# Where a fused attention and MLP kernel forms z and kv: at a step of their own, or at the head of the runs of sketches and numerators

## The chip, the cores and the metric

The kernel runs on one core of a Trainium2 chip. Its time is the device time of one execution in microseconds; 260.84 us is the median of three runs of the kernel before (260.82 to 261.14). One execution was also profiled. Engines are named as in the profile: PE is TensorE (PEld its weight loads), DVE is VectorE, ACT is ScalarE, POOL is GpSimd, SP is SyncE, which issues the DMAs.

## The reference

A linear attention with sketched second-order features, followed by an MLP with an exact GELU. Batch 4, heads 4, sequence 1088, head size 32, sketch size 8, hidden size 2048:

```python
a = einsum('rd,bhsd->bhsr', S1, x); b = einsum('rd,bhsd->bhsr', S2, x)
phi(x) = a_i * b_j                        # 8 x 8 = 64 features a token
kv  = einsum('bhsf,bhsd->bhfd', phi(k), v)   # per batch and head: 64 x 32
z   = sum over s of phi(k)                   # per batch and head: 64
num = phi(q) @ kv ;  den = phi(q) @ z + 1e-6
x   = num / den, heads side by side          # 4352 tokens x 128
out = gelu(x @ w_in) @ w_out                 # 128 -> 2048 -> 128
```

## The kernel before

The queries are handled in chunks of 512 tokens: chunk n is half of the first 1024 tokens of batch n // 2, eight chunks in all, and a ninth chunk (n = 8) holds the 64 last tokens of all four batches. The MLP is a list of steps `(n, fi)`: step t makes 128 hidden channels of one chunk (`hidden`, L686 to L699: TensorE into one of two PSUM banks `h_ps`, then the GELU on ScalarE). From step 32 on, chunk n has the sixteen steps 16 n to 16 n + 15. Four hidden blocks in a row form a block, for which GpSimd makes sums (`token_sums`, L741 to L744), and one or more steps later TensorE multiplies blocks and sums by `w_out` (`two_products`, L776), seven products in place of eight. When a chunk's products are done, VectorE and ScalarE take them from PSUM (`drain`, L788 to L797), and VectorE combines and turns them for the store (`combine` and `store`, L810 to L838).

Attention work is written into slots between these steps: `at(t, f, ...)` puts f behind the hidden step of t and ahead of the products of t. Each engine runs its instructions in the order of this text, by manual dependences between neighbours; nothing is reordered by a scheduler. For batch b from 1 on and chunk n the work is:

- `key_turn_blocks`, `features_of_all`, `outer_of_all`, `add_tokens`: the features `k_p` of the batch's keys and, on VectorE, their sums over eight tokens a lane, `k_s` (L969 to L975).
- `kv_sum` (L431): 36 matmuls with 128 rows and 32 columns, kv of each head transposed, one head in each quarter of the array. `z_sum` (L440): four matmuls of the same shape, `ones` against `k_s`, which put z of each head on its 32 lanes.
- `take_kv` (ScalarE copy) and `turn_kv` (two matmuls at 128 rows x 64 columns against the identity, then a ScalarE copy into `kz[b]`), for the numerators.
- `fold_z` calls `sketch_of_z` (L480): three short VectorE instructions contract z with the second sketch matrix and write the result into `S_abc[b]`, the stationary matrix of the query sketches.
- `query_turn(n)`, `query_sketch(n)` (L557: eight matmuls with 64 rows and 32 columns, `S_abc[b]` against the turned queries), `query_outer(n)` (L574: on VectorE, a, b and the denominator give the features divided by the denominator).
- `attend(n)` (L605): eight matmuls at 64 rows x 32 columns, `kz[b]` against the features; ScalarE copies the result to `xT`, which the hidden steps of chunk n multiply.

Batch 0 has a way of its own before the steps begin; its z is only needed in the form of `S_abc[0]` for the ninth chunk. `repeat_first_z` (slot 40) lays it out as `z_cols` on GpSimd (L496), and `turn_first_kv` turns it on TensorE and folds it.

The loop over n from 3 on puts the work in relation to t = 16 (n - 1), the first step of chunk n - 1. Before the change, kv and z of batches 2 and 3 stand together (`finish_keys` at t + 13 for n = 3 and 5), with the first z's turn behind them for batch 2, and `turn_kv` and the fold one slot later; two slots after kv, at t + 15, come the numerators of the chunk whose steps begin next and the sketch of the chunk after it (chunks 3 and 4 for batch 2). For batch 1, kv stands at slot 21, its turn at 22, z and its fold at 23, and the sketch of chunk 2 at 24.

Each call of `work_banks` takes the next of two pairs of PSUM banks (`w_ps`), and waits until what used that pair two calls ago is done.

Of the kernel before, what the change touches and what calls it, by code (L numbers as in the profile page):

```python
# [16 lines left out]
def kernel(  # L17
# [18 lines left out]
    pe, dve, act, pool, sp = nc.tensor, nc.vector, nc.scalar, nc.gpsimd, nc.sync  # L36
    B, H, S, D = q.shape
    R = S1.shape[0]
    F = R * R
# [3 lines left out]
    NP = H // 2  # L43
# [4 lines left out]
    CW = JC * 128  # L48
    G = 128 // 32
    NCH = J // JC  # L50
# [16 lines left out]
    def work_banks():  # L67

        return wps.tile([128, 2, CW], FP, name="w_ps")

    def work_bank():
        return work_banks()[:, 0]
# [7 lines left out]
    def out_bank():  # L80
        return ops.tile([128, CW], FP, name="o_ps")
# [137 lines left out]
    ident = big.tile([128, 128], FP, name="ident")  # L219
# [12 lines left out]
    ones = big.tile([128, D], FP, name="ones")  # L232
# [173 lines left out]
    k_s = {}  # L406

    def flat(features):
        return features.rearrange("p i j -> p (i j)")
# [16 lines left out]
    def kv_product(ps, lhsT, features, h, part, start=False, stop=False):  # L426

        pe.matmul(ps[h * D:(h + 1) * D, part * F:(part + 1) * F], lhsT=lhsT, rhs=features, start=start, stop=stop,  # L428
                  skip_group_check=True)

    def kv_sum(b, ps):  # L431


        for i in range(J):
            for h in range(H):
                kv_product(ps, main["v", b][:, h, i, :], k_p[b][h // 2][:, i, h % 2], h, 0, start=i == 0)
        for h in range(H):
            kv_product(ps, v_rem_aug[b][:, h, :], flat(k_p_rem[b % 2][:, h]), h, 0, stop=True)

    def z_sum(b):  # L440

        ps = held["kv"][:, 0]
        for h in range(H):
            kv_product(ps, ones, k_s[b][:, h], h, 1, start=True, stop=True)

    def fold_z(b):
        sketch_of_z(b, held["kv"][:, 0], F)

    kv_T = {}

    def take_kv(b, ps):
        kv_T[b] = att.tile([128, F], FP, name="kv_T")
        act.copy(out=kv_T[b], in_=ps[:, :F])

    def turn_kv(b, banks):

        for rows in (slice(0, 64), slice(64, 128)):
            pe.matmul(banks[rows, 1, :128], lhsT=kv_T[b], rhs=ident, start=True, stop=True)
        act.copy(out=kz[b], in_=banks[:, 1, :128])
# [20 lines left out]
    def sketch_of_z(b, ps, at):  # L480

        zs = att.tile([128, R, R], FP, name="z_s")
        dve.tensor_mul(out=zs, in0=ps[:, at:at + F].rearrange("p (i j) -> p i j", i=R), in1=sT[:, None, R:].broadcast_to([128, R, R]))
        c = ps[:, 2 * F:2 * F + R]
        dve.tensor_reduce(out=c, in_=zs, axis=mybir.AxisListType.X, op=AX.add)
        dve.tensor_mul(out=S_abc[b][:, :, :, 4:8], in0=c.rearrange("p (i f) -> p i f", i=2)[:, :, None].broadcast_to([128, 2, 2, 4]),
                       in1=own_r[:, None, :, None].broadcast_to([128, 2, 2, 4]))
# [11 lines left out]
    def turn_first_kv():  # L499

        ps, zs = work_bank(), held["zs"]
        for h in range(H):
            c, r = h // 2, h % 2
            pe.matmul(ps[h * D:(h + 1) * D, :F], lhsT=zs[:, r], rhs=ident[:, c * F:(c + 1) * F], start=True, stop=True)
        sketch_of_z(0, ps, 0)


# [44 lines left out]
    def batch_of(n, s, i):  # L552
        return n // NCH if n < NMAIN else i * 2 + s
# [51 lines left out]
    def attend(n, banks=None):  # L605


        W = width[n]
        m = 1 if n < NMAIN else B // 2
        banks = work_banks() if banks is None else banks  # L610
        f = qp[n].rearrange("f r x -> f (r x)")[:, :2 * W].rearrange("f (c i n r t) -> f c i n r t", c=NP, i=m, r=2, t=32)
        N = W // 2 // m
        for i in range(m):
            for s in range(2):
                rows, b = slice(s * 64, (s + 1) * 64), batch_of(n, s, i)
                for h in range(H):
                    pe.matmul(banks[h * D:(h + 1) * D, s, i * N:(i + 1) * N],  # L617
                              lhsT=(kz[b] if b else kz_first)[rows, h * D:(h + 1) * D],
                              rhs=f[rows, h // 2, i, :, h % 2], start=True, stop=True)
        xT[n] = att.tile([128, CW], FP, name="xT", bufs=3)  # L620
        to = xT[n][:, :W]
        to = to.rearrange("p (s x) -> p s x", s=2) if m == 1 else to.rearrange("p (s t i) -> p s i t", s=2, i=m)
        act.copy(out=to, in_=banks[:, :, :W // 2] if m == 1 else banks[:, :, :W // 2].rearrange("p s (i t) -> p s i t", i=m))
# [238 lines left out]
    r = Rounding(SR)  # L862
# [12 lines left out]
    banks = [out_bank(), out_bank()]  # L875
# [59 lines left out]
    def at(t, f, *a):  # L935
        slots[t].append(lambda: f(*a))
# [40 lines left out]
    held = {}  # L977
# [11 lines left out]
    def features_rem(pair):  # L989
        key_features_rem(pair, held["rem"])  # L990

    def finish_keys(b, z=True):
        held["kv"] = work_banks()
        kv_sum(b, held["kv"][:, 0])
        if z:
            z_sum(b)
        take_kv(b, held["kv"][:, 0])

    def round_at(t, w, product_by=dve):
        r = []  # L1000
# [18 lines left out]
    at(17, add_tokens, 1)  # L1019
    at(18, channel_sums, 4)  # L1020

    at(21, finish_keys, 1, False)
    at(22, lambda: turn_kv(1, held["kv"]))
    at(23, z_sum, 1)
    at(23, fold_z, 1)
    at(23, query_turn, 3)
    at(24, query_sketch, 2)
    at(24, query_outer, 2)
    for i, t in enumerate((25, 26, 28)):
        at(t, channel_sums, i)  # L1030
# [2 lines left out]
    for n in range(3, NCHUNK):  # L1033

        t = (n - 1) * NF
        b = (n + 1) // 2
        keys = n % 2 and b < B
        if n > 3:
            at(t - 6, query_turn, n)
        if keys:  # L1040
            at(t - 1, sketch_and_attend, n)
            at(t - 1, features_of_all, b)
        else:
            at(t - 1, attend, n - 1)
            at(t - 1, query_sketch, n)
        at(t - 1, query_outer, n)
        if keys:
            for r in range(2):
                at(t - 3 if n > 3 else t - 4, key_turn_blocks, b, r)

        if n == NMAIN:
            at(t + 15, attend, n)
        if keys:
            at(t + 5 + (n == NCH + 1), outer_of_all, b)
            at(t + 5 + (n == NCH + 1), add_tokens, b)
            at(t + 8, widen_v_rem, b)
            at(t + 13, finish_keys, b)
            if b == 2:
                at(t + 13, turn_first_kv)
            at(t + 14, lambda b=b: turn_kv(b, held["kv"]))  # L1060
            at(t + 14, fold_z, b)


    products = {t: [] for t in range(len(steps) + LAG)}
# [2 lines left out]
    for t, (n, fi) in enumerate(steps):  # L1067
# [13 lines left out]
        elif fi % NB == NB - 1:  # L1081
            b = fi // NB
# [11 lines left out]
    for t in range(len(steps) + LAG):  # L1094
        if t < 4:
# [9 lines left out]
            if t == 3:  # L1105
                banks = work_banks()
# [23 lines left out]
        if t < len(steps):  # L1130
            n, fi = steps[t]
            hidden(n, fi, by_halves=t >= 18 and (n < NMAIN or fi < 5))
        if t < len(steps) and steps[t][0] < NMAIN and steps[t][1] % NB == NB - 1:
            n, b = steps[t][0], steps[t][1] // NB
# [50 lines left out]
```

## Time and profile before

| | |
|---|---|
| median of the runs | 260.84 us |
| profiled execution | 260.86 us |
| span of the profiled execution | 259.1 us |
| clock granted to TensorE | 0.999 |
| `kv_sum` and `z_sum` (L428), first and last start | 51.3 and 151.5 us |
| sketches (L568) of chunks 2 to 7, first and last start | 57.1 and 183.2 us |
| numerators (L617) of chunks 2 to 7, first start | 69.0 us |
| fold of z (L483, L485, L486), median of each instruction | 224, 228 and 174 ns |

The span runs from the first to the last instruction that the profiler saw; the time of an execution is some 1.8 us longer. A row of the timeline gives the start, the length, the engine and line, what is written from what, the tile of the array (rows*columns) and the shape, and the number of rows merged (each fp32 matmul shows as two passes). Neighbouring passes overlap, so the cost of a group is read from its start to the start of the next group, and not from its length. A bracket at the end gives idle time before it and what ended that time.

### The profile page before, as it was taken

The page shows a single profiled execution, that of the slowest core. Times are in us where ns is not written, and L with a number is a line of the kernel's source. Part 1 is how long each engine was busy: PE and PEld are TensorE (multiplying, and loading weights), DVE is VectorE, ACT ScalarE, POOL GpSimd, SP SyncE. Part 2 cuts the span into 40 slices and gives each one's busy share as a digit, 9 for nine tenths or more (in the row PEclk, how much of TensorE's full clock was granted, in tenths as well). Part 3 has the DMA queues.
Part 4 walks back from the last instruction along what each step waited for, and adds up shares of the span by engine and source line. Part 5 has one row for each costly group of instructions (what it writes and reads, how often), then busy time and mean ns, then how long its engine had stood idle before and what let it go on. Part 6 is the DMA issues. An engine that isn't in the chain of part 4 may idle for free.

```text
span 259.1 us, 5758 instructions
## 1 busy us (share of the span) xinstructions
PE 254.6 (98%) x2335; PEld 134.8 (52%) x2335; DVE 151.6 (59%) x313; ACT 114.9 (44%) x221; POOL 163.5 (63%) x173
## 2 busy tenths in 40 slices
PE   8999999999999999999999999999999999999994
PEld 7856444344444554444444454444445444445794
DVE  2886879969698997680178957630565043600330
ACT  4675767432625333533335334533353335334431
POOL 3404006799968776687758766867768776877200
PEclk9999999999999999999999999999999999999999
DMA  6469849820000101001000011020001100010020
GB/s 205 137 192 360 206 95 220 217 54 13 3 0 13 30 4 28 13 12 31 3 0 3 0 27 17 3 41 0 3 0 25 19 4 0 14 29 0 3 41 20
DMA packets 29530, 13.48 MB, mean 52 GB/s; under 512 B 21824, under 2 KB 27712, under 8 KB 29504
## 3 DMA queue, kind: packets, MB, share of 16 engines
q1 hardware_dynamic: 29472, 13.12, 20.8%
q8 instruction: 18, 0.29, 0.5%
q14 instruction: 8, 0.07, 0.1%
q10 hardware_dynamic: 32, 0.00, 0.0%
HBM read 10.88 MB, written 2.23 MB: 51 GB/s over the span
## 4 chain that ended last, share of the span: by engine, by line
PE 98%; ACT 0%; issue 0%; DVE 0%
PE h_ps L692 45%; PE o_ps L776 33%; PE o_ps L827 5%; PE w_ps L824 3%; PE w_ps L428 2%; PE w_ps L857 1%; PE w_ps L617 1%; PE w_ps L568 1%; PE o_ps L417 1%; PE w_ps L534 1%; PE h_ps L706 1%; PE h_ps L333 1%; PE w_ps L945 1%; PE w_ps L635 0%; PE w_ps L333 0%; PE h_ps L373 0%
## 5 line engine op out<-in xcount | busy, mean ns | idle before, releaser
L692 PE MATMUL h_ps<-xT,w_in 128*64 128x512 f32 (+3 forms) x514 | 137.1, 576 | 0.0
L699 ACT ACTIVATE block<-h_ps 128x512 f32<-128x512 f32 (+1 forms) x128 | 73.0, 571 | 120.2 <-PE h_ps L692 119.8
L776 PE MATMUL o_ps<-block,w_out 128*64 128x256 f32 x224 | 57.5, 379 | 0.0
L692 PEld LDWEIGHTS h_ps<-xT,w_in 128*64 128x64 f32 (+1 forms) x514 | 41.9, 142 | 29.2 <-issue 11.6
L741 POOL TENSOR_TENSOR bits_low<-block 128x512 f32<-128x512 f32 x28 | 35.6, 1273 | 27.6 <-ACT block L699 27.6
L776 PEld LDWEIGHTS o_ps<-block,w_out 128*64 128x64 f32 x224 | 30.5, 137 | 37.5 <-issue 26.7
L742 POOL TENSOR_TENSOR bits_a<-block 128x512 f32<-128x512 f32 x28 | 35.7, 1276 | 12.8 <-ACT block L699 12.8
L743 POOL TENSOR_TENSOR bits_e<-bits_a,block 128x512 f32<-128x512 f32 x28 | 36.1, 1290 | 2.2
L744 POOL TENSOR_TENSOR bits_m<-block,bits_e 128x512 f32<-128x512 f32 x28 | 35.8, 1280 | 2.2
L580 DVE STREAM_TRANSPOSE w_ps<-w_ps 128x512 f32<-128x512 f32 (+1 forms) x7 | 4.9, 693 | 42.8 <-PE w_ps L568 30.1
L776 PE MATMUL o_ps<-bits_low,small 128*64 128x256 f32 x112 | 29.0, 381 | 0.0
L776 PE MATMUL o_ps<-block,small 128*64 128x256 f32 x112 | 28.9, 381 | 0.0
L776 PE MATMUL o_ps<-bits_a,small 128*64 128x256 f32 x112 | 28.8, 379 | 0.0
L776 PE MATMUL o_ps<-bits_m,w_out 128*64 128x256 f32 x112 | 28.7, 379 | 0.0
L776 PEld LDWEIGHTS o_ps<-block,small 128*64 128x64 f32 x112 | 15.0, 137 | 17.6 <-issue 10.2
L791 DVE COPY sums<-o_ps 64x256 f32<-64x256 f32 x8 | 3.3, 416 | 34.4 <-PE o_ps L776 34.4
L776 PE MATMUL o_ps<-bits_e,small 128*64 128x256 f32 x112 | 17.1, 384 | 0.0
L827 PE MATMUL o_ps<-g,w_out 128*128 128x512 f32 (+1 forms) x34 | 16.5, 572 | 0.0
L776 PEld LDWEIGHTS o_ps<-bits_m,w_out 128*64 128x64 f32 x112 | 15.3, 137 | 0.0
L776 PEld LDWEIGHTS o_ps<-bits_a,small 128*64 128x64 f32 x112 | 15.2, 137 | 0.0
L776 PEld LDWEIGHTS o_ps<-bits_low,small 128*64 128x64 f32 x112 | 15.0, 137 | 0.0
L776 PEld LDWEIGHTS o_ps<-bits_e,small 128*64 128x64 f32 x112 | 7.5, 136 | 10.6 <-issue 9.1
(181 smaller groups left out, 303.2 us busy)
## 6 DMA issues: line engine op xcount, KB each, us to landing
out_dram<-oT SPq DMA_DIRECT2D x26, 64.0 KB, 2.2
block<-in_moe_w_in_dram SPq DMA_DIRECT2D x3, 512.0 KB, 7.2
block<-in_moe_w_out_dram SPq DMA_DIRECT2D x3, 512.0 KB, 11.6
k<-in_k_dram SPq DMA_DIRECT2D x12, 128.0 KB, 2.8
v<-in_v_dram SPq DMA_DIRECT2D x12, 128.0 KB, 3.4
q<-in_q_dram SPq DMA_DIRECT2D x24, 64.0 KB, 2.3
k<-in_k_dram SPq DMA_DIRECT2D x2, 256.0 KB, 2.8
q<-in_q_dram SPq DMA_DIRECT2D x2, 256.0 KB, 4.1
```

What stands on the lines that cost most here:

```text
L428: pe.matmul(ps[h * D:(h + 1) * D, part * F:(part + 1) * F], lhsT=lhsT, rhs=features, start=start, stop=stop, skip_group_check=True)
L580: dve.transpose(out=tok, in_=ps[:, :, :H2])
L692: pe.matmul(ps[rows, :W], lhsT=w[:, rows], rhs=xT[n][:, :W], start=True, stop=True)
L699: act.activation(out=g_of[n, fi][:, :W], in_=ps[:, :W], func=ACT.Gelu)
L741: pool.tensor_sub(out=s[3], in0=a11, in1=a21)
L742: pool.tensor_add(out=s[1], in0=a21, in1=a22)
L743: pool.tensor_sub(out=s[2], in0=s[1], in1=a11)
L744: pool.tensor_sub(out=s[4], in0=a12, in1=s[2])
L776: pe.matmul(acc[n][bank][half * 64:(half + 1) * 64, col:col + HW], lhsT=fixed, rhs=moving, start=opens and e == 0 and name in "4715", stop ...
L791: dve.tensor_copy(out=N[lo, 0, one], in_=a0[lo, one])
L824: pe.matmul(o_of[n][i][:, :128], lhsT=g[:, i * 128:(i + 1) * 128], rhs=w_tile(w_out_sb, fi), start=first, stop=final)
L827: pe.matmul(o_of[n][:, cols], lhsT=w_tile(w_out_sb, fi), rhs=g[:, cols], start=first, stop=final)
```

## The change

Three things are changed. z and kv of batches 1 to 3 move to the head of the run that holds the numerators and the sketch: z first, then its fold on VectorE, then kv, then (for batches 2 and 3) the numerators of the chunk before, then the sketch. z gets a pair of banks of its own, and kv and the numerators share one pair: kv lies in the second half of the second bank. `turn_kv` moves to two slots after kv. The first z's turn takes two matmuls with 64 columns in place of four with 32, and stands three slots earlier, alone. (In the changed file, L503 is the first z's turn.)

```diff
     def z_sum(b):
-        ps = held["kv"][:, 0]
+        held["z"] = work_bank()
         for h in range(H):
-            kv_product(ps, ones, k_s[b][:, h], h, 1, start=True, stop=True)
+            kv_product(held["z"], ones, k_s[b][:, h], h, 0, start=True, stop=True)
     def fold_z(b):
-        sketch_of_z(b, held["kv"][:, 0], F)
+        sketch_of_z(b, held["z"], 0)
...
     def turn_first_kv():
         ps, zs = work_bank(), held["zs"]
-        for h in range(H):
-            c, r = h // 2, h % 2
-            pe.matmul(ps[h * D:(h + 1) * D, :F], lhsT=zs[:, r], rhs=ident[:, c * F:(c + 1) * F], start=True, stop=True)
+        for c in range(NP):
+            pe.matmul(ps[c * F:(c + 1) * F, :F], lhsT=zs.rearrange("f r d -> f (r d)"), rhs=ident[:, c * F:(c + 1) * F],
+                      start=True, stop=True)
         sketch_of_z(0, ps, 0)
...
-    def finish_keys(b, z=True):
-        held["kv"] = work_banks()
-        kv_sum(b, held["kv"][:, 0])
-        if z:
-            z_sum(b)
-        take_kv(b, held["kv"][:, 0])
+    def kv_and_attend(b, n):
+        banks = held["kv"] = work_banks()
+        kv_sum(b, banks[:, 1, CW // 2:])
+        if n >= NCH:
+            attend(n, banks)
+        take_kv(b, banks[:, 1, CW // 2:])
...
-    at(21, finish_keys, 1, False)
-    at(22, lambda: turn_kv(1, held["kv"]))
-    at(23, z_sum, 1)
-    at(23, fold_z, 1)
+    at(24, z_sum, 1)
+    at(24, fold_z, 1)
     at(23, query_turn, 3)
+    at(24, kv_and_attend, 1, 1)
     at(24, query_sketch, 2)
+    at(26, lambda: turn_kv(1, held["kv"]))
     at(24, query_outer, 2)
...
     for n in range(3, NCHUNK):
         t = (n - 1) * NF
-        b = (n + 1) // 2
+        b = (n + 1) // 2 if n % 2 else n // 2
         keys = n % 2 and b < B
...
         else:
-            at(t - 1, attend, n - 1)
+            if n % 2 == 0 and b < B:
+                at(t - 1, z_sum, b)
+                at(t - 1, fold_z, b)
+                at(t - 1, kv_and_attend, b, n - 1)
+                at(t + 1, lambda b=b: turn_kv(b, held["kv"]))
+            else:
+                at(t - 1, attend, n - 1)
             at(t - 1, query_sketch, n)
...
             at(t + 8, widen_v_rem, b)
-            at(t + 13, finish_keys, b)
             if b == 2:
-                at(t + 13, turn_first_kv)
-            at(t + 14, lambda b=b: turn_kv(b, held["kv"]))
-            at(t + 14, fold_z, b)
+                at(t + 10, turn_first_kv)
```

## The prediction

> **What bounds the kernel now.** I read the page first: shares by engine, then the chain of waits.
>
> ```profile
> PE 254.6 (98%) x2335; PEld 134.8 (52%) x2335; DVE 151.6 (59%) x313; ACT 114.9 (44%) x221; POOL 163.5 (63%) x173
> PE 98%; ACT 0%; issue 0%; DVE 0%
> ```
>
> TensorE is busy for 98% of the span and is 98% of the chain; no other engine has a share. So only what makes TensorE's stream of matmuls shorter, or puts a hole into it, counts. The profiled execution took 260.86 us, its span 259.1; the median of the runs shown is 260.84, so sums made against the profile carry over as they are.
>
> Busy is not streaming, so next I read TensorE's timeline around batch 2's kv, by start times: the distance from one start to the next is what a group costs.
>
> ```profile
> 93.31 1.03 PE L692 MATMUL h_ps<-xT,w_in 128*64 128x512 f32 x4
> 94.26 1.10 PE L428 MATMUL w_ps<-k_p,v 128*32 128x64 f32 x64
> 95.18 0.29 PE L428 MATMUL w_ps<-k_p_rem,v_rem_aug 128*32 128x64 f32 x8
> 95.29 0.29 PE L428 MATMUL w_ps<-k_s,ones 128*32 128x64 f32 x8
> 95.40 0.29 PE L504 MATMUL w_ps<-ident,z_cols 128*32 128x64 f32 x8
> 95.63 0.43 PE L776 MATMUL o_ps<-block,small 128*64 128x256 f32 x1
> ...
> 95.89 0.38 PE L776 MATMUL o_ps<-block,small 128*64 128x256 f32 x1
> ...
> 97.40 0.39 PE L458 MATMUL w_ps<-ident,kv_T 128*64 128x128 f32 x4
> 97.62 0.38 PE L776 MATMUL o_ps<-block,w_out 128*64 128x256 f32 x1
> ...
> 98.48 1.03 PE L692 MATMUL h_ps<-xT,w_in 128*64 128x512 f32 x4
> 99.44 0.66 PE L617 MATMUL w_ps<-q_pT,kz 64*32 64x256 f32 x16
> 99.90 0.64 PE L568 MATMUL w_ps<-qT,S_abc 64*32 64x256 f32 x16
> 100.47 0.65 PE L776 MATMUL o_ps<-bits_e,small 128*64 128x256 f32 x4
> 100.95 1.03 PE L692 MATMUL h_ps<-xT,w_in 128*64 128x512 f32 x4
> ```
>
> Undisturbed, a hidden step (L692 x4) takes 0.86 us, a pair of products 0.215 and eight passes at 128x32 0.11. The rest is paid at each change of tile shape. For kv: 0.10 before it (94.26 - 93.31 - 0.86, rounded up), 0.04 in its first group (0.92 for 64 passes that would need 0.88), 0.11 after its last (95.63 - 95.40 - 0.11), 0.045 in the next product: 0.295. For the 64x32 run: 0.10 before, 0.03 in the first group (0.46 against 0.43), 0.135 after (0.57 against 0.43), 0.045 in the next product: 0.31.
>
> **What the Trainium skill says.** "TensorEngine Tiling (Array Packing)", section Tiling Modes, says that a change of the tiling mode, unlike a change of tile, drains TensorE. The trace agrees: attend and sketch use eight tiles of one shape with nothing lost between them, and each change of shape costs the above. "SBUF — State Buffer", section Who interferes with whom, says that a VectorE instruction with two SBUF inputs and a GpSimd instruction that reads SBUF lock each other out for a whole instruction. The trace agrees: L811 takes 1.41 us beside L744, and 0.42 as its median.
>
> **The change part by part.** Call a stay in another shape an excursion.
>
> *Batch 1.* Before: kv (128x32), z (128x32) and the sketch (64x32) are three excursions at 51.2, 54.4 and 57.0: 0.295 + 0.285 (0.10 + 0.14 + 0.045 around z) + 0.31 = 0.89. After: one run 128x64 to 128x32 to 64x32 to 128x64. Entry 0.10 + 0.04, exit 0.135 + 0.045, and in the middle a change from 128x32 to 64x32 that no row of before shows. Bounds: nothing if tiles that only split their rows needn't drain; 0.20 if it is a little dearer than any seen. The nearest row changes the rows alone, from 64x64 to 32x64: L635's first 32 passes take 0.49 us (start 12.11 to 12.60), the second 32 take 0.57 before L534 at 13.17, with the drain. At 0.014 each that is 0.12 of drain. I take 0.12 + 0.03 of slow first passes = 0.15. The run then costs 0.47, saved 0.42.
>
> *Batches 2 and 3.* Two excursions each, 0.605, become one of 0.47: 0.135 each. Saved in all 0.42 + 0.27 = 0.69. The passes of z and kv, the numerators, the sketches and turn_kv (0.22, 97.40 to 97.62) are the same in number; turn_kv stays at 128x64 between a hidden step and products.
>
> *The first z's turn.* Its eight passes cost 0.11 inside kv's run. Now four at 128x64 stand alone between a hidden step and products, in the shape of their neighbours. Bounds: 0.11, as in kv's run, and 0.22, as L458's four passes of twice the columns. L399's four 64-column passes at 128x64 took 0.16 (10.00 to 10.16); I take that: 0.05 dearer. It reads z_cols, which GpSimd finishes at 88.42; the turn comes after the hidden step that starts at 88.57, at 89.43: covered by 1.0 us.
>
> *Hidden steps without cover.* In batch 1, before, kv stands between the fourth and fifth of six hidden steps that have no products between them, and gives ScalarE time. After, all six run back to back. ScalarE is behind there:
>
> ```profile
> 50.52 0.60 ACT L699 ACTIVATE block<-h_ps 128x512 f32<-128x512 f32 x1 [0.40 <-PE h_ps L692]
> 51.01 0.58 ACT L804 COPY g<-o_ps 128x512 f32<-128x512 f32 x1
> 51.48 0.62 ACT L699 ACTIVATE block<-h_ps 128x512 f32<-128x512 f32 x1
> ```
>
> There are two hidden banks. The fifth step would start at 51.17 and waits for the activation that ends at 51.12, the sixth at about 52.13 for that which ends at 52.10. From such an end to the next matmul took 0.15 (49.26 to 49.41). So 0.10 + 0.14 = 0.24 lost, between 0.1 and 0.4. GpSimd's sums are in time even so: bits_e, needed about 1.7 us earlier than the 55.66 of before, is done at 53.21.
>
> *The fold.* Before, VectorE's three instructions that make S_abc from z lie far ahead of the sketch. Now the sketch waits for them with only kv (and attend) between.
>
> ```profile
> 54.96 0.22 DVE L483 TENSOR_TENSOR z_s<-w_ps,sT 128x64 f32<-128x64 f32 x1 [0.92 <-PE w_ps L428]
> 55.21 0.23 DVE L485 TENSOR_REDUCE w_ps<-z_s 128x8 f32<-128x64 f32 x1
> 55.55 0.17 DVE L486 TENSOR_TENSOR S_abc<-w_ps,own_r 128x16 f32<-128x16 f32 x1
> ```
>
> z's first matmul was at 54.50, so with R as the run's start the fold begins at R + 0.46 and ends at R + 1.22. In batch 1 TensorE reaches the sketch at R + 0.04 + 0.11 + 0.99 (72 passes of kv) + 0.12 = R + 1.26; with 0.11 from an end to a weight load (49.26 to 49.37) the sketch can start at R + 1.33. Lost 0.08; bounds 0 and 0.3. Queued behind the waiting sketch are all later products and hidden steps. The turn of chunk 3's queries, now ahead of the fold on VectorE, runs from 54.04 to 54.75, before z's end. In batch 3 VectorE is idle from 151.9 and attend adds 0.46: no wait. In batch 2 VectorE has a backlog: k_s ends at 93.05, then the first z's fold (now 0.70 earlier in the queue), the query turn, L810, L811, L813 and the output turn, which ended at 97.84. Moved by at most 0.70 it ends at 98.54. The run starts at about 98.48 - 1.505 (kv's stay) - 0.22 (turn_kv) + 0.16 + 0.96 = 97.9, z is ready for the fold at 98.4, the fold ends near 99.25, the sketch is due at 99.6. No wait, with 0.3 to spare.
>
> *Other queues.* SP and GpSimd issue the same in the same order. ScalarE copies xT before kv_T, so the next hidden step waits as before: xT ended at 100.79, its weight load came at 100.85.
>
> **Sum.** 0.69 saved - 0.05 - 0.24 - 0.08 = 0.32 us. 260.86 - 0.32 = 260.54; I say 260.5, 0.1% faster.
>
> **Rivals.**
> 1. *Shape changes are cheaper than I price them, or the stalls don't come.* With the middle change free 0.45 more is saved; with half the two stalls 0.16. 260.86 - 0.32 - 0.45 to - 0.61: 259.9 to 260.1. For it: nothing measures this change. Against: the rows-only change drained too.
> 2. *The holes eat it all.* If the hidden steps lose 0.4 and the sketch 0.25, the gain is 0.69 - 0.05 - 0.65, nothing: 260.9. For it: ScalarE's queue is full just there.
> 3. *Slower, by the fold of batch 2.* If VectorE comes to L813 (two SBUF inputs) after GpSimd has begun the next L741, about 97.0 in the new order, it is locked out for 1.27 us, the output turn ends at about 99.6, the fold at 100.3, and the sketch due at 99.6 stands for 0.8 us: 260.54 + 0.8 = 261.3, and 261.6 if batch 1's fold is late by 0.3 too. It decides as soon as L813 starts 0.6 us later than before (96.41). For it: a 0.70 us fold is put ahead in this very queue, and L810 and L811 are already slowed. Against: L810 waits for GpSimd anyway until 94.67, which swallows the move.
>
> That the change doesn't do what it says is excluded: the new program has z, kv, numerators and sketch next to one another.
>
> **How the numbers follow.** Forecast (260.2 to 260.8) 0.48, rival 1 0.25, rival 2 0.13, rival 3 and other waits 0.14. Predicted 260.5. The range leaves out a tenth on each side: 259.9 to 261.2. No change means within 0.2%, 0.52 us, about what can be told here: 260.32 to 261.36. Faster: rival 1 and the lower edge of the forecast, 0.29. Slower: the upper part of rival 3, 0.11. Within: 0.60.
>
> **What will show it.** Right: from the first kv matmul's last group to attend's first start some 0.12 us more than the passes need; batch 1's sketch start less than 0.1 us behind the drain; VectorE's fold of batch 2 ended before attend has been issued. Wrong: attend right behind kv without a gap, or a weight load of the sketch that waits for VectorE for more than 0.3 us, or a hole in the hidden steps of batch 1 of over 0.4.

## The result and the profile after

The changed kernel takes 260.4 us in the median (259.74 to 260.87), the kernel before, measured together with it, 260.81; the ratio is 0.9983, with a 95% interval of 0.9976 to 0.9991. That is 0.43 us less, 0.17%. Measured once more, in a later set of runs, it gave 0.9982 (0.9974 to 0.9990).

The page's shares by engine, and its chain of waits:

```profile
PE 254.2 (98%) x2331; PEld 135.0 (52%) x2331; DVE 150.8 (58%) x313; ACT 114.8 (44%) x221; POOL 163.6 (63%) x173
PE 98%; ACT 0%; issue 0%; DVE 0%
```

TensorE has four passes fewer and is as full as before; nothing else has come into the chain. The span fell from 259.1 to 258.6 us. The start-up takes a little different time in every execution: the first hidden step at 128x64 begins at 47.53 us in the profile before and at 47.62 in the one after. So I measure from that step to the start of the last projection (L824, x16). That stage took 206.16 us before and 205.63 after: 0.53 us less. In a second profile of the changed kernel it took 205.63 again; the kernel before was profiled once.

TensorE's timeline around batch 1 (start, length, engine and line, tile, shape, rows merged):

```profile
47.62 5.69 PE L692 MATMUL h_ps<-xT,w_in 128*64 128x512 f32 x24
53.14 0.38 PE L776 MATMUL o_ps<-block,small 128*64 128x256 f32 x1
...
54.44 1.03 PE L692 MATMUL h_ps<-xT,w_in 128*64 128x512 f32 x4
55.39 0.32 PE L428 MATMUL w_ps<-k_s,ones 128*32 128x64 f32 x8
55.53 1.08 PE L428 MATMUL w_ps<-k_p,v 128*32 128x64 f32 x64
56.42 0.29 PE L428 MATMUL w_ps<-k_p_rem,v_rem_aug 128*32 128x64 f32 x8
56.69 0.67 PE L568 MATMUL w_ps<-qT,S_abc 64*32 64x256 f32 x16
57.29 0.43 PE L776 MATMUL o_ps<-block,w_out 128*64 128x256 f32 x1
```

and around batch 2:

```profile
88.43 1.03 PE L692 MATMUL h_ps<-xT,w_in 128*64 128x512 f32 x4
89.29 0.28 PE L503 MATMUL w_ps<-ident,z_cols 128*64 128x64 f32 x4
89.41 0.38 PE L776 MATMUL o_ps<-block,w_out 128*64 128x256 f32 x1
...
96.73 1.03 PE L692 MATMUL h_ps<-xT,w_in 128*64 128x512 f32 x4
97.68 0.32 PE L428 MATMUL w_ps<-k_s,ones 128*32 128x64 f32 x8
97.82 1.08 PE L428 MATMUL w_ps<-k_p,v 128*32 128x64 f32 x64
98.71 0.29 PE L428 MATMUL w_ps<-k_p_rem,v_rem_aug 128*32 128x64 f32 x8
98.94 0.66 PE L617 MATMUL w_ps<-q_pT,kz 64*32 64x256 f32 x16
99.39 0.64 PE L568 MATMUL w_ps<-qT,S_abc 64*32 64x256 f32 x16
99.96 0.65 PE L776 MATMUL o_ps<-bits_e,small 128*64 128x256 f32 x4
100.44 1.03 PE L692 MATMUL h_ps<-xT,w_in 128*64 128x512 f32 x4
```

The new change of shape is the step from kv's last group to the numerators. Eight passes need 0.11 us, and the next group starts 0.23 after (98.71 to 98.94): 0.12 of drain, the time in which TensorE starts nothing because the shape changes, and 0.02 more in the numerators' first passes. In batch 1 the step is 0.27 (56.42 to 56.69): the same drain and some 0.045 of waiting for the fold. The fold's last instruction and the sketch's weight loads, 0.12 after its end at 56.54:

```profile
56.37 0.17 DVE L486 TENSOR_TENSOR S_abc<-w_ps,own_r 128x16 f32<-128x16 f32 x1
56.66 0.21 PEld L568 LDWEIGHTS w_ps<-qT,S_abc 64*32 64x32 f32 x16
```

What lies around the matmuls of a run is then, for batch 1, 57.29 + 0.045 - 55.30 - 1.53 = 0.505 (the hidden step ends at 54.44 + 0.86 = 55.30, and 1.53 is what z, kv and the sketch need), against 0.89 in three excursions. For batch 2 it is 0.45, against 0.605; batch 3, read in the same way (153.48 to 156.34), has 0.46.

The first z's turn takes 0.12 us (89.29 to 89.41). The six hidden steps of batch 1 take 5.52 (47.62 to 53.14). Before, the first four took 3.64 (47.53 to 51.17), and two more would be 1.72: 0.16 is lost.

The gain adds up: 0.385 + 0.155 + 0.145 saved, less 0.01 for the turn and 0.16 for the hidden steps, is 0.515 of the 0.53.

### The profile page after: what moved, and what is told of

The parts are those of the page before. It is cut to its first block, busy times and chain, and to the rows that moved or that the text cites. A ratio compares the mean times of both kernels' runs of the same rounds, so it can differ in the third digit from the quotient of the medians.

```text
span 258.6 us, 5749 instructions
## 1 busy us (share of the span) xinstructions
PE 254.2 (98%) x2331; PEld 135.0 (52%) x2331; DVE 150.8 (58%) x313; ACT 114.8 (44%) x221; POOL 163.6 (63%) x173
## 3 DMA queue, kind: packets, MB, share of 16 engines
HBM read 10.88 MB, written 2.23 MB: 51 GB/s over the span
## 4 chain that ended last, share of the span: by engine, by line
PE 98%; ACT 0%; issue 0%; DVE 0%
PE h_ps L692 45%; PE o_ps L776 33%; PE o_ps L827 5%; PE w_ps L824 3%; PE w_ps L428 1%; PE w_ps L857 1%; PE w_ps L617 1%; PE w_ps L568 1%; PE o_ps L417 1%; PE w_ps L534 1%; PE h_ps L706 1%; PE h_ps L333 1%; PE w_ps L945 1%; PE w_ps L635 0%; PE w_ps L333 0%; PE h_ps L373 0%
## 5 line engine op out<-in xcount | busy, mean ns | idle before, releaser
L741 POOL TENSOR_TENSOR bits_low<-block 128x512 f32<-128x512 f32 x28 | 35.8, 1279 | 27.7 <-ACT block L699 27.7
L743 POOL TENSOR_TENSOR bits_e<-bits_a,block 128x512 f32<-128x512 f32 x28 | 36.1, 1291 | 2.2
```

Of the source, the lines that this page charges most:

```text
L741: pool.tensor_sub(out=s[3], in0=a11, in1=a21)
L743: pool.tensor_sub(out=s[2], in0=s[1], in1=a11)
```

## Experiments

A ratio stands against the kernel before, measured in the same set of runs; the bracket behind it is its 95% interval. The stage is that of the last section, read from each kernel's profile.

### Batch 1 alone, and all but batch 1

The first kernel puts batch 1's work back:

```diff
-    at(24, z_sum, 1)
-    at(24, fold_z, 1)
...
+    at(21, first_keys)
+    at(22, lambda: turn_kv(1, held["kv"]))
+    at(23, first_z)
+    at(23, lambda: sketch_of_z(1, held["kv"][:, 0], F))
     at(23, query_turn, 3)
-    at(24, kv_and_attend, 1, 1)
     at(24, query_sketch, 2)
-    at(26, lambda: turn_kv(1, held["kv"]))
```

`first_keys` (kv and its copy) and `first_z` write to one bank, as before the change.

> Batch 1 as before the change, the rest changed. Theory (each run of 128x32 and 64x32 work that is joined to another saves the changes of shape, about 0.15 us in batches 2 and 3, and about 0.38 in batch 1 less 0.16 lost between its hidden steps): gain over the kernel before 0.29 us of the 0.52 seen between the two profiles, so a profiled span of about 258.8 and no hole between the fourth and sixth hidden step near 51. Rival (batch 1's gain is eaten by the hidden steps, all of the gain is in batches 2 and 3): the same time as the changed kernel. Rival (the gain lies in z's own banks or in the earlier first turn, not in the shapes): also the same as the changed kernel.

Measured: 260.62 us in the median, 0.9990 (0.9982 to 0.9998). The stage took 205.86, 0.30 less than before. kv follows the fourth hidden step at 51.16, as it did.

The second kernel is the one before with the opposite edit: batch 1's z, fold, kv and turn at slots 24 and 26, z in its own banks, kv in the second half of a bank, and nothing else.

> Only batch 1 changed, all else as before, the first z's turn too. Theory: gain 0.22 us over the kernel before, all of it between 47 and 61 us. Rival (batch 1's gain is eaten by the hidden steps): no gain.

Measured: 260.31, 0.9986 (0.9979 to 0.9994). The stage took 205.93, 0.23 less. The two parts make 0.53, which is the whole. So batch 1's gain isn't eaten, and it doesn't come from the early turn of the first z, which this kernel lacks. It does have z in banks of its own, and so have batches 2 and 3 of the first kernel: no run separates this rival. But the profile before leaves it nothing to save: in batch 2 z follows kv's last group after 0.11, its bare passes (95.18 to 95.29), and in batch 1 it follows the hidden step after 0.10 (54.40 to 54.50), the price of the shape. The sum over changes of shape leaves nothing for it either. In the medians the two parts stand the other way round, 0.18 below the kernel before for the first kernel and 0.49 for the second. The two intervals overlap and hold the stages' 0.30 and 0.23, so the split rests on the stages, of which there is one profile for each kernel.

### The price of a change of shape

The first z's turn at its new place, with 32 columns:

```diff
-        for c in range(NP):
-            pe.matmul(ps[c * F:(c + 1) * F, :F], lhsT=zs.rearrange("f r d -> f (r d)"), rhs=ident[:, c * F:(c + 1) * F],
-                      start=True, stop=True)
+        for h in range(H):
+            c, r = h // 2, h % 2
+            pe.matmul(ps[h * D:(h + 1) * D, :F], lhsT=zs[:, r], rhs=ident[:, c * F:(c + 1) * F], start=True, stop=True)
```

> As changed, with the first z's turn in four matmuls with 32 columns at its new place, where its neighbours have 64. Theory: a stay of its own in another shape: 0.10 + 0.03 + 0.11 + 0.11 + 0.045, about 0.40 us from the hidden step's end to the products against 0.12: 0.28 us more. Rival (so short a stay hides behind the weight loads of its neighbours): 0.12 as with 64 columns.

TensorE's timeline of it:

```profile
88.45 1.03 PE L692 MATMUL h_ps<-xT,w_in 128*64 128x512 f32 x4
89.41 0.32 PE L504 MATMUL w_ps<-ident,z_cols 128*32 128x64 f32 x8
89.66 0.43 PE L776 MATMUL o_ps<-block,w_out 128*64 128x256 f32 x1
...
89.92 0.38 PE L776 MATMUL o_ps<-block,w_out 128*64 128x256 f32 x1
```

From the hidden step's end (89.31) it takes 0.35 to the products, and the first product 0.26 in place of 0.215: 0.395 against 0.12. The stage took 205.91, 0.28 more than the changed kernel; the median was 260.57, 0.9990 (0.9982 to 0.9998). The same passes, whose share inside a run of their own shape was 0.11, cost 0.28 us more where they stand alone. This is what the 64 columns of the changed kernel avoid.

The next run was to double the change between 128x32 and 64x32, by putting kv between the numerators and the sketch:

```diff
-        kv_sum(b, banks[:, 1, CW // 2:])
         if n >= NCH:
             attend(n, banks)
+        kv_sum(b, banks[:, 1, CW // 2:])
```

> As changed, but in batches 2 and 3 the numerators stand between z and kv: two more changes between 128x32 and 64x32 in each run, the same matmuls. Theory: each change costs 0.14 us, 0.28 a batch, 0.56 us in all over the changed kernel: about 261.0, no gain left. In the timeline 0.11 to 0.12 between the last passes of one shape and the first of the next. Rival (such a change is nearly free, since only the rows are split): less than 0.1 us.

Measured: 262.41, 1.0065 (1.0050 to 1.0081), the stage 2.23 longer than in the changed kernel. Neither theory had this:

```profile
97.29 0.32 PE L428 MATMUL w_ps<-k_s,ones 128*32 128x64 f32 x8
97.54 0.66 PE L617 MATMUL w_ps<-q_pT,kz 64*32 64x256 f32 x16
98.95 1.10 PE L428 MATMUL w_ps<-k_p,v 128*32 128x64 f32 x64 [0.74 <-ACT xT L623]
99.87 0.29 PE L428 MATMUL w_ps<-k_p_rem,v_rem_aug 128*32 128x64 f32 x8
100.09 0.66 PE L568 MATMUL w_ps<-qT,S_abc 64*32 64x256 f32 x16
```

kv now waits until ScalarE has copied the numerators, whose second bank it shares (in another half of its columns, but this program orders the two by bank): it starts at 98.95, and by its passes and drain it would have started at about 98.11 (97.54 + 0.46 + 0.11). That is 0.84 of the 1.12 us by which each of the two runs is longer; the rest is the two changes. Two of them can still be read: z to numerators, 0.25 for eight passes that need 0.11 and whose first group costs 0.03 more, so 0.11; kv to sketch, 0.22 for eight passes, so 0.11. It also shows why kv stands ahead of the numerators in the shared banks.

So the doubling was tried again without that wait: z a second time, into an idle bank of its own pair, between the numerators and the sketch of batches 2 and 3:

```diff
+    def z_again(b):
+        for h in range(H):
+            kv_product(held["z2"][:, 1], ones, k_s[b][:, h], h, 0, start=True, stop=True)
...
                 at(t - 1, kv_and_attend, b, n - 1)
+                at(t - 1, z_again, b)
```

> As changed, with z of batches 2 and 3 made a second time, into an idle bank, between the numerators and the sketch: eight passes at 128x32 and two more changes of shape (64x32 to 128x32 and back) in each run, and no new wait for another engine. The earlier run that was to double these changes was confounded by a wait for ScalarE. Theory: 0.11 for the passes and 0.14 for each change, 0.39 a batch, 0.78 in all over the changed kernel: about 261.2. Rival (a change that only splits the rows is nearly free): the passes alone, 0.22 in all, about 260.6.

Measured: 261.49, 1.0026 (1.0019 to 1.0033), the stage 1.15 longer than in the changed kernel, 0.57 in each run:

```profile
98.58 0.66 PE L618 MATMUL w_ps<-q_pT,kz 64*32 64x256 f32 x16
99.17 0.32 PE L428 MATMUL w_ps<-k_s,ones 128*32 128x64 f32 x8
99.58 0.67 PE L569 MATMUL w_ps<-qT,S_abc 64*32 64x256 f32 x16
```

and its weight loads:

```profile
98.58 0.18 PEld L618 LDWEIGHTS w_ps<-q_pT,kz 64*32 64x32 f32 x16
99.17 0.16 PEld L428 LDWEIGHTS w_ps<-k_s,ones 128*32 128x32 f32 x8 [0.41 <-issue]
99.58 0.18 PEld L569 LDWEIGHTS w_ps<-qT,S_abc 64*32 64x32 f32 x16 [0.25 <-PE w_ps L428]
```

From the numerators to z there is 0.59 for what needs 0.46: 0.13 of drain. From z to the sketch there is 0.41; 0.11 are the passes and 0.14 what such a change and the slow first passes cost elsewhere, and the bracket names a further wait: the sketch's pair of banks is the one that z has just written, and TensorE waits there for its own matmuls to end. That is the 0.16 to 0.18 a run beyond the 0.39 expected; it is what is left over, and no run measures it alone. The free change is refuted; the total isn't a clean measure of its price, but the step from the numerators to z is.

### How much the fold may be late

> As changed, with the fold of z done twice in a row in batches 1 to 3, the result being the same: 0.68 us more on VectorE ahead of the sketch. Theory: in batch 1 nothing covers it, the sketch comes about 0.65 later; in batches 2 and 3 the fold was done 0.42 us ahead of the sketch's weight loads, so about 0.35 each is exposed (0.68 less 0.42, and 0.1 for the wait). In all about 1.3 us, 261.7. Rival (VectorE has more to spare than that, since TensorE's own matmuls hold the sketch): no change in batches 2 and 3, 0.65 in all.

```diff
     def fold_z(b):
         sketch_of_z(b, held["z"], 0)
+        sketch_of_z(b, held["z"], 0)
```

Measured: 261.2, 1.0017 (1.0008 to 1.0025), the stage 0.90 longer than in the changed kernel: 0.60 in batch 1, 0.15 to 0.16 each in batches 2 and 3. Batch 1 is nearly as expected, the others show less than half. The fold of batch 2 on VectorE, its second time, in this kernel (the edit moves line numbers behind it by one), and then TensorE's weight loads:

```profile
98.77 0.21 DVE L484 TENSOR_TENSOR z_s<-w_ps,sT 128x64 f32<-128x64 f32 x1
99.01 0.23 DVE L486 TENSOR_REDUCE w_ps<-z_s 128x8 f32<-128x64 f32 x1
99.28 0.17 DVE L487 TENSOR_TENSOR S_abc<-w_ps,own_r 128x16 f32<-128x16 f32 x1
```

```profile
99.02 0.18 PEld L618 LDWEIGHTS w_ps<-q_pT,kz 64*32 64x32 f32 x16
99.57 0.21 PEld L569 LDWEIGHTS w_ps<-qT,S_abc 64*32 64x32 f32 x16 [0.37 <-issue]
```

The loads come 0.12 after the fold's end, 99.45, and the sketch's matmul 0.03 after the loads, at 99.60. (The bracket of these loads names no releaser; in batch 1 of this kernel the bracket of the sketch names the fold, 0.58 us <-DVE S_abc L487.) In the changed kernel the loads of the sketch ran 0.21 ahead of it (99.18 and 99.39). I had counted the cover up to the loads; they run ahead only because they can, and that lead is cover too. The fold of the changed kernel ended at 98.76, so it had 0.63 to the sketch, less 0.15 for the way to it: 0.48. The second fold was also shorter than the 0.68 that I took: it began 0.62 after the first (98.15 and 98.77), and S_abc was ready 0.61 later after z's start than in the changed kernel. 0.61 - 0.48 is 0.13, which with 0.02 to 0.03 in the sketch's first passes makes the 0.15 to 0.16.

### Where the hidden steps lose time, and a faster version

```diff
-                slots[t + LAG + 1 + 2 * n].append(lambda n=n: take_usual(n))
+                slots[t + LAG + 1 + 4 * n].append(lambda n=n: take_usual(n))
```

> As changed, with ScalarE's copy of the second out bank two steps later, so that the fourth hidden step's activation comes at once. Theory: the copy puts that activation back by about 0.1 us, and the sixth hidden step waits for it: 0.05 to 0.1 us gained between 47.6 and 53.1, products there at about 53.05. Rival (the sixth step waits because ScalarE's way from a hidden step's end to its bank being free is longer than two steps, with or without the copy): less than 0.03 us.

ScalarE's timeline of the changed kernel, with the loads of the fifth and sixth hidden step:

```profile
50.60 0.60 ACT L699 ACTIVATE block<-h_ps 128x512 f32<-128x512 f32 x1 [0.40 <-PE h_ps L692]
51.09 0.58 ACT L804 COPY g<-o_ps 128x512 f32<-128x512 f32 x1
51.56 0.62 ACT L699 ACTIVATE block<-h_ps 128x512 f32<-128x512 f32 x1
...
51.25 0.20 PEld L692 LDWEIGHTS h_ps<-xT,w_in 128*64 128x64 f32 x4 [0.71 <-ACT block L699]
52.23 0.20 PEld L692 LDWEIGHTS h_ps<-xT,w_in 128*64 128x64 f32 x4 [0.78 <-ACT block L699]
```

and of the one with the later copy:

```profile
51.36 0.60 ACT L699 ACTIVATE block<-h_ps 128x512 f32<-128x512 f32 x1 [0.26 <-PE h_ps L692]
52.28 0.60 ACT L699 ACTIVATE block<-h_ps 128x512 f32<-128x512 f32 x1 [0.32 <-PE h_ps L692]
52.77 0.58 ACT L804 COPY g<-o_ps 128x512 f32<-128x512 f32 x1
```

The fourth step's activation now follows its matmuls, and the copy lies behind the fifth's, where no hidden step needs it. The six steps took 5.40 (47.52 to 52.92) in place of 5.52, the stage 205.51, 0.12 less than in the changed kernel and more than the 0.05 to 0.1 expected; the rival is refuted. The median was 260.24, 0.9975 (0.9964 to 0.9986).

Both were run once more with the kernel before on one chip:

> The changed kernel with the later copy once more, beside the kernel before on the same chip: 0.65 us below it between the first of the six hidden steps and the end, as its first profile shows.

> The changed kernel itself, beside the two others on the same chip: 0.53 us below the kernel before from the first of the six hidden steps to the end, and 0.12 above the one with the later copy.

Measured: 260.07, 0.9971 (0.9962 to 0.9981), stage 205.52, for the later copy; 260.46, 0.9982 (0.9974 to 0.9990), stage 205.63, for the changed kernel. The stages are 0.64 and 0.53 below the kernel before. The later copy with the change has the shortest stage here, twice, and the lowest median. The two medians differ by 0.39, more than the stages do, but the intervals hold the stages' differences.

## Why the prediction was right, point by point

- *The bound.* TensorE stayed at 98% of the chain, and every tenth of a microsecond was found between its groups.
- *The change from 128x32 to 64x32*, taken as 0.15 between 0 and 0.20 from a row that only changes the rows elsewhere: 0.12 of drain and 0.02 in the next group. The Trainium skill's sentence in "TensorEngine Tiling (Array Packing)", section Tiling Modes, that a change of mode drains TensorE and a change of tile doesn't, holds here for a split of the rows alone too: 0.11 to 0.13 at each such change, while numerators and sketch, of one mode, still follow each other at 0.45 with no drain between them. The cheap change of rival 1 is refuted; its other half, smaller stalls, came in part: 0.205 of the 0.32 forecast.
- *What the shapes save.* 0.42 and twice 0.135 were forecast, 0.69; measured 0.43 (with the wait for the fold taken out), 0.155 and 0.145, 0.73. What is left of the difference is in readings of 0.01 to 0.02.
- *The first z's turn.* Forecast 0.05 dearer, measured 0.01: the four passes take 0.12, near the lower bound. The nearest row that I took, L399's 0.16, was too dear.
- *The hidden steps.* The mechanism was right and the place of it too, as the later copy shows; the size was 0.16 and not 0.24. The term mis-sized is the way from an activation's end to the next hidden step. I took 0.15 from one row; in the changed kernel it is 0.05 both times, 51.20 to 51.25 and 52.18 to 52.23. So the fifth step's wait of 0.10 wasn't there to that extent: its loads start where the four steps before it end (51.26), and 0.04 is what stays when the copy is moved. The sixth step's 0.14 came out about right, 0.12, by luck: the shorter way is made up by the sooner end of the fifth step, and by a step that takes 0.91 and not 0.86 where its loads haven't run ahead (52.23 to 53.14), which I hadn't counted.
- *The fold.* In batch 1 it costs 0.045 (forecast 0.08, which my own sum, 1.33 less 1.26, makes 0.07; between 0 and 0.3). It began 0.39 after the run's start (55.39 to 55.78) where I took 0.46, and ended at 1.15 in place of 1.22. In batch 2 I gave it 0.3 to spare, and it had 0.48. VectorE's queue there, in the changed kernel, and behind it GpSimd's:

```profile
93.77 0.71 DVE L519 STREAM_TRANSPOSE qT<-q 128x512 f32<-128x512 f32 x1
94.41 0.53 DVE L810 TENSOR_TENSOR sums<-sums 64x256 f32<-64x256 f32 x1
94.95 1.41 DVE L811 TENSOR_TENSOR sums<-sums 64x256 f32<-64x256 f32 x1
96.39 0.69 DVE L813 TENSOR_TENSOR sums<-sums,g 128x512 f32<-128x512 f32 x1
97.11 0.71 DVE L838 STREAM_TRANSPOSE oT<-sums 128x512 f32<-128x512 f32 x1
98.07 0.23 DVE L483 TENSOR_TENSOR z_s<-w_ps,sT 128x64 f32<-128x64 f32 x1 [0.25 <-PE w_ps L428]
...
93.38 1.28 POOL L743 TENSOR_TENSOR bits_e<-bits_a,block 128x512 f32<-128x512 f32 x1
...
96.76 1.46 POOL L741 TENSOR_TENSOR bits_low<-block 128x512 f32<-128x512 f32 x1 [0.69 <-ACT block L699]
```

  The first z's fold came ahead and L810 started 0.69 later than before; yet L811 starts at 94.95 in place of 94.96. L810's length fell from 1.23 to 0.53: the time it had stood beside GpSimd's L743 swallowed the move, which is the reason given against rival 3. L813 starts at 96.39 (before: 96.41), ahead of GpSimd's L741, so rival 3 didn't occur. It was nearer than I thought: L741 begins at 96.76 and not at about 97.0, which left 0.37 us and not 0.6. Had the fold been late all the same, it would have cost less than I said, by the cover that the lead of the weight loads gives.
- *Rival 2* named the right holes; with the 0.01 of the first z's turn they took 0.215 of 0.73 instead of all.
- *The sum.* Forecast 0.32 saved, measured 0.53 in the stage and 0.43 in the medians. The saving was nearly right; it is the three costs, 0.37 forecast and 0.215 measured, that were each taken too high, and the 0.04 of the saving on top. These errors all lie on one side, so none of them cancelled in the sum; the gain in the stage was taken too small by 0.21.
- *The signs.* The three that were named for being right all came: 0.12 between kv and the numerators, a sketch 0.045 behind the drain in batch 1, and in batch 2 a fold that ended at 98.76, ahead of the numerators at 98.94.

## What to carry to other kernels

On a TensorE that is the bound, count the changes of tile shape in its order and price each from start to start: here one cost 0.10 to 0.14 us of drain, with 0.02 to 0.05 in the group behind it, whether rows, columns or both changed, so small matmuls of a rare shape belong together, or in the shape of their neighbours. When work is moved away, look at what it had covered: two hidden steps lost 0.16 us, of which 0.12 went when a ScalarE copy was moved out of their way. And before a small group is put between others in shared banks, ask who reads those banks: a shared bank turned a 0.6 us experiment into one of 2.2.

## What was not expected of the hardware

- Weight loads that run ahead are a reserve. A matmul whose loads came late started 0.03 us after them (99.57 to 99.60), against 0.21 when they had run ahead; a fold that ended 0.61 us later cost 0.15 where I had worked out 0.35 for 0.68.
- TensorE can wait for itself: in one run a group that goes into a bank which the group just before it has written stood for 0.16 to 0.18 us beyond the drain and its passes. The program's order asks for that wait; what it would take without it was not measured.
- The stage behind the start-up repeats to 0.01 us between profiles of one kernel (205.63 twice, 205.51 and 205.52), while the start-up itself moved the first 128x64 hidden step between 46.92 and 47.74 us. What lies outside the start-up and the stage took 7.16 to 7.20 us in all eleven profiled executions, so between these the times differ by start-up and stage alone. Single times of one kernel spread by about 1 us; that the start-up makes that spread too is likely, but most of these executions have no profile.
